# Attention and two feed-forward nets on one core: the head's chunks, weight fetches and one weight's last two steps rearranged

## The chip, the core and the metric

One core of a Trainium2 chip runs one program. Its engines are TensorE (PE; its weight loads PEld), VectorE (DVE), ScalarE (ACT), GpSimd (POOL) and SyncE (SP), which issues nearly all of the transfers. The metric is the device time of one execution in microseconds (us); lower is better.

## The reference

```python
qn = q / (np.linalg.norm(q, axis=1, keepdims=True) + 1e-06)   # q, k, v: 1 x 6016 x 256
kn = k / (np.linalg.norm(k, axis=1, keepdims=True) + 1e-06)
s = kn.transpose(0, 2, 1) @ qn / tau                          # 256 x 256
a = softmax(s, -1)
x = v @ a                                                     # 6016 x 256
h = x @ w_in                                                  # 256 -> 2048
g = where(h >= 1, h, where(h <= -1, 0, (h + 1) ** 2 / 4))
x = g @ w_out                                                 # 2048 -> 256
xn = x / sqrt(mean(x * x, -1) + 1e-06) * rms_g
out = (silu(xn @ w_gate) * (xn @ w_val)) @ w_out2             # 256 -> 1536 -> 256
```

The weights are float64 in memory; q, k and v are float32.

## The kernel before

**The head** reads q and k once. The 6016 tokens are 47 rows of 128, read in chunks (`QK_CHUNKS`, L24), each by one transfer of q and one of k (`load_chunk`, L364). For each row PE makes two fp32 products of 256 columns (`scores`, L353; halves b = 0 and 1 of the 256 x 256 score matrix); the trace has two records for each. In the same time the sums of squares of q and k are made: ACT squares a chunk (step `q5` of the table `HEAD`; `head_step`, L378), DVE adds the squares into the four rows of `acc` (`+5`, L400); at the end two folds, `<2` and `<1` (L405), leave one row, and four small products with a column of ones (`norm_ps`, L444) sum it over the partitions.

The head also turns the first three pieces of `w_in` (`wide`, 512 KB each; `fetch` after the chunks named by `FETCH_AT`) from float64 to a float32 pair, high and low part. A piece takes seven steps, written in `HEAD` as digit and letter: `c` clamp (DVE, L245), `h` shift (ACT, L252), `s` sign (DVE, L262), `r` rescale (ACT, L269), `j` join (DVE, L282), `u` high part (ACT, L321), `l` low part (DVE, L177). `2j 2u 2l` are the last three of the third piece. `HEAD` is the order of DVE and ACT in the head, `SCORES` that of PE, and each engine works its list strictly in order.

**Behind the head** a list scheduler at the end of the function orders everything, by costs and due times of its own: first the chain of the softmax (`softmax`, L570). ACT takes the square root of the norms (`norms_q`, L586), DVE the reciprocal and a diagonal matrix `rq` (L594), PE multiplies it out (`rq_ps`, L599), then come scaling, exponential, transposes and the product of the attention matrix with `w_in` (`product_w1`, L785), so that `v` goes straight into `x @ w_in` (`block_A`, L819; matmuls L830). The piece `s_ps` of the scores is copied by ACT (`s_sb`, L602) just ahead of `norms_q`. The scheduler starts with one clock for each engine (L1376), its assumption of when the engine is free of the head.

**The first net** (`block_A`, `squared`, `block_B`) follows at once, while the rest of the weights is still being turned: `soon`, the three pieces whose transfers go first after the head, and `wide_...`. In `squared` ACT and DVE make `g` from `h`, ACT the high part `gh`, DVE the low part `gl`; `block_B` multiplies both with `wo`, a piece of `w_out` with its own high and low part (`to_rows`, L718), in three matmuls: `gh` with the high part, `gh` with the low part, `gl` with the high part. A low part (`low`, L532; recorded as L177, `sub_hi`) can also be given to POOL, where the scheduler expects it to end earlier there than on DVE and the due time is below `SWAP_UNTIL`. From then on the same pattern goes through six pairs of token tiles and both nets.

Of the kernel before, what the change touches and what calls it, by code (L numbers as in the profile page):

```python
# [8 lines left out]
F32 = mybir.dt.float32  # L9
# [7 lines left out]
P = 128  # L17
TOK = 512
# [2 lines left out]
QK_BUFS = 8  # L21
SQ_BUFS = 3

QK_CHUNKS = (2, 2, 4, 4, 4, 4, 4, 4, 4, 4, 4, 3, 2, 2)  # L24
OWN = 2
ROWS = 4

WARM = 4
FILL = 12.0
NORM_AFTER = (11, 1)  # L30
SCORES = (
    (0, 0), (0, 1), (1, 0), (1, 1), (2, 0), (2, 1), (3, 0), (3, 1), (4, 0), (4, 1), (5, 0), (5, 1),
    (6, 0), (6, 1), (7, 0), (7, 1), (8, 0), (9, 0), (8, 1), (10, 0), (11, 0), (9, 1), (12, 0),
    (13, 0), (10, 1), (11, 1),
)
HEAD = (
    "q0 q1 q2 +2 q3 +3 0h 0c q4 0s 0r +4 1h 0j q5 1c 1s 0u +5 q6 1r 0l 2h +6 q7 1j 2c 1u +7 q8 1l +8 "
    "q9 2s +9 2r t q10 2j T 2u +10 q11 2l +11 q12 +12 q13 +13 <2 <1"
).split()

EARLY = 3
FETCH_AT = (3, 4, 6)

ORDER = ((1, 0), (1, 1), (2, 0), (1, 2), (2, 1), (1, 3), (2, 2), (1, 4), (2, 3), (1, 5), (2, 4), (2, 5))
PAIR = (1.5, 16.5)
# [46 lines left out]
def tile_channel_attention_two_ffn(  # L92
# [128 lines left out]
    def load_v(t):  # L221
        v_in[t] = op_slot(5 + t, [P, NC, TOK], F32, f"vin{t}")
        n0, n = tiles[t]
        nc.sync.dma_start(
            out=by_token(v_in[t]), in_=v[0, n0:n0 + n, :].rearrange("(m p) c -> p m c", p=P))
# [191 lines left out]
    with in_order(ENG.PE, ENG.DVE, ENG.Activation, ENG.SP):  # L417
        keep_warm(WARM)
        for ci in range(NQ):
            old = ci - QK_BUFS  # L420
            if 0 <= old and ci < NQ - OWN:
                for todo, upto, do in (
                    (steps, f"q{old}", head_step), (products, (old, 1), lambda w: scores(*w)),
                ):
                    while upto in todo:
                        do(todo.pop(0))
            load_chunk(ci)
            if ci == 0:
                nc.scalar.activation(out=seen, in_=ones[:, :1], func=AF.Sqrt)
            if ci == NQ // 2:  # L430
                nc.sync.dma_start(out=tau_sb, in_=tau.broadcast_to([P, 1]))
            if ci in FETCH_AT:
                fetch()
        load_v(0)
        load_v(1)
        while steps:
            head_step(steps.pop(0))
        sums = acc[:, :, 0]
        while products:
            scores(*products[0])  # L440
            if products.pop(0) == NORM_AFTER:
                for a in range(2):
                    for b in range(NC):
                        nc.tensor.matmul(  # L444
                            norm_ps[a][:, 2 * b:2 * b + 2], sums[:, a, b * P:(b + 1) * P],
                            ones[:, :2], start=True, stop=True,
                        )
    sent = {}
    for i, src in zip((2, 3, 4), SOON):
        x = op_slot(i, [P, NC, TOK], F32, f"soon{i}")  # L450
        sent[id(src)] = i, x

# [90 lines left out]
    def given(cls, name, slot, t, when=0.0):  # L543
        b = Buf(cls, name, slot=slot)
        b.t, b.when = t, when
        held.append(b)
        return b
# [92 lines left out]
        return ([rq_ps, rq_ps], mx_b[1:] * NC, s_b[0]), ([rq_ps, mx_b[1]], (), None)  # L640

    w1_part = Buf(None, "w1")

    vt_buf = {(t, c): Buf(None, f"vt{t}_{c}") for t in range(2) for c in range(NC)}
    for b, x in zip(vt_buf.values(), (s_all[1][1], s_all[0][0], warm, s_all[1][0])):
# [34 lines left out]
    def narrow(key, src, at, step, into=None):  # L680
        x = Buf("op", f"wide_{key}", [P, NC, TOK])
        low, high = (x, 0), (x, 1)
        if id(src) in sent:
            i, t = sent[id(src)]
            x = given("op", x.name, i, t, -10.0)
            low, high = (x, 0), (x, 1)
            op("SP", (0.5, 1.5), lambda: dma_wide(x.t, src), i - 100.0, writes=[low, high])
        else:
            op("SP", dma(512), lambda: dma_wide(x.t, src), at - LEAD["wide"], writes=[low, high], new=[x])
        small = pool(TOK * POOL_TS_NS / 1000)  # L690
        op("DVE", dve_fast(TOK), lambda: clamp(x.t), at, writes=[high],
           other=None if id(src) in sent else ("POOL", small, lambda: clamp(x.t, nc.gpsimd)))
        op("ACT", act(TOK), lambda: shift_act(x.t), at, writes=[low],
           other=("DVE", dve_fast(TOK), lambda: shift_dve(x.t)))
        op("DVE", dve(TOK), lambda: sign(x.t), at + step, [high], [low])
        op("ACT", act(TOK), lambda: rescale(x.t), at + step, [low], [high],
           other=("DVE", dve_fast(TOK), lambda: rescale_dve(x.t)))
        if into is None:
            op("DVE", dve(TOK), lambda: join(x.t), at + 2 * step, [high], [low])
        else:  # L700
            op("DVE", dve(TOK), lambda: join(
                x.t, into.t[:, :4, :].rearrange("p s c -> p (s c)")),
                at + 2 * step, [low, high], [(into, s) for s in range(4)], [into])
        return x
# [666 lines left out]
    for o in order:  # L1371
        o.new = [b for b in {id(b): b for b, _, _ in o.uses}.values() if b.cls and b.t is None]
        for b in o.new:
            if b not in queue[b.cls]:
                queue[b.cls].append(b)
    clock = {"PE": 1.2, "ACT": -2.6, "DVE": 0.0, "POOL": 0.0, "SP": -10.0}  # L1376
    dma_free = -4.9
    pending = {e: [] for e in clock}
    for o in order:
# [177 lines left out]
```

## Time and profile before

| | |
|---|---|
| median of three runs | 1098.97 us (1098.47 to 1099.27) |
| profiled execution, its own time | 1098.53 us |
| its span | 1096.7 us |
| DVE busy | 840.8 us, 77% |
| ACT busy | 799.8 us, 73% |
| POOL busy | 107.5 us, 10% |
| DMA over the span | 204.36 MB, 186 GB/s |

A row of the timeline has start, length (both us), engine, line, operation, what it writes and reads with shapes, and in brackets the idle time just before it and what ended that. Matmuls overlap, so the distance of two starts tells their pace, not their length. The page counts PE as busy nearly throughout; what matters is when it waits and in which order the other engines reach what it waits for.

### The profile page before, as it was taken

The page shows a single profiled execution, that of the slowest core. Times are in us where ns is not written, and L with a number is a line of the kernel's source. Part 1 is how long each engine was busy: PE and PEld are TensorE (multiplying, and loading weights), DVE is VectorE, ACT ScalarE, POOL GpSimd, SP SyncE. Part 2 cuts the span into 40 slices and gives each one's busy share as a digit, 9 for nine tenths or more (in the row PEclk, how much of TensorE's full clock was granted, in tenths as well). Part 3 has the DMA queues.
Part 4 walks back from the last instruction along what each step waited for, and adds up shares of the span by engine and source line. Part 5 has one row for each costly group of instructions (what it writes and reads, how often), then busy time and mean ns, then how long its engine had stood idle before and what let it go on. Part 6 is the DMA issues. An engine that isn't in the chain of part 4 may idle for free.

```text
span 1096.7 us, 14304 instructions
## 1 busy us (share of the span) xinstructions
PE 1090.2 (99%) x5038; PEld 923.2 (84%) x5038; DVE 840.8 (77%) x1342; ACT 799.8 (73%) x1454; POOL 107.5 (10%) x116
## 2 busy tenths in 40 slices
PE   9999999999999999999999999999999999999998
PEld 7888888888888888888888888998888888998887
DVE  5999999969999568867667967667967666866454
ACT  7799998877679776667877657887556877565553
POOL 0022213304222002000000200000100000200000
PEclk9999999999999999999999999999999999999999
DMA  9993576845688744446554445765455534455531
GB/s 360 368 304 124 184 256 232 226 155 198 218 302 240 197 158 133 163 170 194 149 152 163 150 169 132 231 174 170 143 172 129 196 135 167 159 179 161 187 115 39
DMA packets 130519, 204.36 MB, mean 186 GB/s; under 512 B 87184, under 2 KB 89232, under 8 KB 130448
## 3 DMA queue, kind: packets, MB, share of 16 engines
q1 hardware_dynamic: 129760, 202.80, 57.6%
q8 instruction: 40, 0.66, 0.2%
q10 hardware_dynamic: 688, 0.66, 0.2%
q14 instruction: 31, 0.25, 0.1%
HBM read 171.57 MB, written 31.85 MB: 185 GB/s over the span
## 4 chain that ended last, share of the span: by engine, by line
PE 97%; DMA 2%; DVE 1%; SPq 0%; issue 0%; DVEq 0%
PE y L868 23%; PE o L1091 14%; PE gx L989 9%; PE vx L989 9%; PE h L830 8%; PE hx L989 8%; PE gy L989 4%; PE vy L989 4%; PE hy L989 4%; PE o L1099 3%; PE s_ps L356 2%; PE vz L989 2%; PE gz L989 2%; PE hz L989 2%; DMA qk<-in_k_dram 2%; PE w_ps L798 1%
## 5 line engine op out<-in xcount | busy, mean ns | idle before, releaser
L868 PE MATMUL y<-gh,wo 128*128 128x512 f32 (+1 forms) x768 | 233.5, 385 | 0.0
L868 PEld LDWEIGHTS y<-gh,wo 128*128 128x128 f32 x768 | 144.2, 188 | 27.1
L177 DVE TENSOR_TENSOR gl<-g,gh 128x512 fp32r<-128x512 f32 (+1 forms) x190 | 128.0, 679 | 28.3 <-ACT gh L529 28.2
L868 PE MATMUL y<-gl,wo 128*128 128x512 f32 (+1 forms) x384 | 148.0, 385 | 0.0
L1091 PE MATMUL o<-uh,wd 128*128 128x512 f32 (+1 forms) x480 | 145.6, 385 | 0.0
L847 ACT ACTIVATE g<-g 128x512 f32<-128x512 f32 (+1 forms) x192 | 117.8, 620 | 1.6
L529 ACT ACTIVATE gh<-g 128x512 fp32r<-128x512 f32 (+1 forms) x192 | 116.9, 618 | 0.1
L1091 PEld LDWEIGHTS o<-uh,wd 128*128 128x128 f32 x480 | 90.1, 188 | 16.7
L1091 PE MATMUL o<-ul,wd 128*128 128x512 f32 (+1 forms) x240 | 92.2, 384 | 0.0
L868 PEld LDWEIGHTS y<-gl,wo 128*128 128x128 f32 x384 | 72.1, 188 | 13.8 <-DVE gl L177 0.4
L915 POOL TENSOR_SCALAR m<-sb 128x16 f32<-128x16 f32 (+1 forms) x12 | 5.1, 422 | 587.3 <-DVE sb L913 587.1
L989 PE MATMUL vx<-xb,vw 128*128 128x512 f32 (+1 forms) x216 | 60.2, 387 | 0.1
L989 PE MATMUL gx<-xb,gw 128*128 128x512 f32 (+1 forms) x216 | 60.1, 386 | 0.0
L989 PE MATMUL vx<-xt,vw 128*128 128x512 f32 (+1 forms) x216 | 59.9, 386 | 0.0
L989 PE MATMUL gx<-xt,gw 128*128 128x512 f32 (+1 forms) x216 | 59.9, 385 | 0.0
L989 PE MATMUL vy<-xt,vw 128*128 128x512 f32 (+1 forms) x216 | 59.9, 385 | 0.0
L989 PE MATMUL gy<-xt,gw 128*128 128x512 f32 (+1 forms) x216 | 59.8, 385 | 0.0
L1002 DVE TENSOR_TENSOR hc<-hy,hc 128x512 f32<-128x512 f32 (+1 forms) x32 | 21.5, 673 | 45.6 <-PE hy L989 45.6
L989 PE MATMUL hx<-vt,hw 128*128 128x512 f32 (+1 forms) x192 | 52.8, 383 | 0.0
L989 PE MATMUL hy<-vt,hw 128*128 128x512 f32 (+1 forms) x192 | 52.8, 383 | 0.0
L177 DVE TENSOR_TENSOR ul<-s,uh 128x512 fp32r<-128x512 f32 (+1 forms) x70 | 47.8, 684 | 6.4 <-ACT uh L529 6.2
L989 PE MATMUL hx<-vb,hw 128*128 128x512 f32 (+1 forms) x192 | 52.5, 383 | 0.0
(235 smaller groups left out, 2476.2 us busy)
## 6 DMA issues: line engine op xcount, KB each, us to landing
gw<-kept_g SPq DMA_DIRECT2D x36, 896.0 KB, 4.5
vw<-kept_v SPq DMA_DIRECT2D x36, 896.0 KB, 4.7
hw<-kept_h SPq DMA_DIRECT2D x32, 896.0 KB, 4.7
wo<-kept_wo SPq DMA_DIRECT2D x40, 512.0 KB, 4.1
wd<-kept_wd SPq DMA_DIRECT2D x36, 512.0 KB, 3.5
qk<-in_q_dram SPq DMA_DIRECT2D x9, 512.0 KB, 9.0
qk<-in_k_dram SPq DMA_DIRECT2D x9, 512.0 KB, 9.0
vin<-in_v_dram SPq DMA_DIRECT2D x32, 128.0 KB, 5.6
```

Source lines behind the costliest of these rows:

```text
L177: return eng.tensor_tensor(out=dst_lo, in0=src, in1=hi.bitcast(F32), op=ALU.subtract)
L356: nc.tensor.matmul(s_ps[b], x[:, 1, j, b * P:(b + 1) * P], x[:, 0, j, :], start=(ci == 0 and j == 0), stop=(ci == NQ - 1 and j == nj - 1),)
L529: op("ACT", act(n), lambda: nc.scalar.activation(out=hi(), in_=src(), func=AF.Copy), at, reads, writes, new, urgent, ("DVE", dve_fast(n), ...
L798: nc.tensor.matmul(got[b].t[:, :n], x[:, c * P:(c + 1) * P], w[:, c, cols], start=(j == 0), stop=(j == len(terms) - 1),)
L830: nc.tensor.matmul(ps.t[:, :n], w[:, c, f * P:(f + 1) * P], x[:, c, :n], start=(i == 0), stop=(i == len(terms) - 1),)
L847: op("ACT", act(n), lambda: nc.scalar.activation(out=r.t[:, :n], in_=r.t[:, :n], func=AF.Square), at, [], [r], urgent=rush)
L868: nc.tensor.matmul(y.t[c][:, :n], w.t[:, f % 2, h, cs], x[:, :n], start=(nth == 1 and i == 0), stop=(nth == NF1 and i == 2),)
L915: nxt("POOL", pool(0.3), lambda: nc.gpsimd.tensor_scalar(out=m.t[:, :nb], in0=s1.t[:, :n].rearrange("p (b j) -> p b j", j=32)[:, :, 0], sc ...
L989: nc.tensor.matmul(ps.t[:, :n], w.t[:, h, a, :], b.t[:, e, :n], start=(start and i == 0), stop=(i == 2), skip_group_check=True,)
L1002: op("DVE", dve(n), lambda: nc.vector.tensor_tensor(out=d.t[:, :n], in0=b.t[:, :n], in1=d.t[:, :n], op=ALU.add), at, [b], [d], urgent=20)
L1091: nc.tensor.matmul(o.t[c][:, :n], w.t[:, f % 2, h, cs], x[:, :n], start=(nth == 1 and i == 0), stop=(nth == NF2 and i == 2),)
L1099: nc.tensor.matmul(o.t[c][:, m * C:(m + 1) * C], x[:, (2 * c + m) * P:(2 * c + m + 1) * P], w.t[:, f % 2, h, :], start=(nth == 1 and i == ...
```

## The change

Four things, all of them numbers in tables or a moved call:

1. The first eight rows come as four chunks of two instead of 2, 2, 4. All later chunks shift by one index, which is most of the difference in `HEAD` and `SCORES`.
2. The three weight pieces are fetched after 16, 24 and 28 rows instead of 8, 12 and 20.
3. The third piece's `2j 2u` go to the end of `HEAD`, behind the folds, and its `2l` goes to the list scheduler, due at 5.0.
4. The first of the three `soon` pieces is sent between the two loads of `v`; the third gets a slot of its own (7). The scheduler's clock for DVE starts at 0.65 instead of 0.

```diff
-QK_CHUNKS = (2, 2, 4, 4, 4, 4, 4, 4, 4, 4, 4, 3, 2, 2)
+QK_CHUNKS = (2, 2, 2, 2, 4, 4, 4, 4, 4, 4, 4, 4, 3, 2, 2)
-    "q9 2s +9 2r t q10 2j T 2u +10 q11 2l +11 q12 +12 q13 +13 <2 <1"
+    "1u 2r q10 1l +10 q11 +11 t q12 +12 q13 +13 q14 T +14 <2 <1 2j 2u"
-FETCH_AT = (3, 4, 6)
+FETCH_AT = (5, 7, 8)
         load_v(0)
+        sent = {id(SOON[0]): (2, op_slot(2, [P, NC, TOK], F32, "soon2"))}
+        dma_wide(sent[id(SOON[0])][1], SOON[0])
         load_v(1)
-    sent = {}
-    for i, src in zip((2, 3, 4), SOON):
+    for i, src in zip((3, 7), SOON[1:]):
     w1_part = Buf(None, "w1")
+    last_wide = given("op", "last_wide", 4, fetched[-1][2], 0.0)
+    op("DVE", dve(TOK), lambda: early_step(EARLY - 1, "l"), 5.0, [last_wide],
+       [(w1_part, (2 * fetched[-1][0] + i, fetched[-1][1])) for i in range(2)])
-            x = given("op", x.name, i, t, -10.0)
+            x = given("op", x.name, i, t, -10.0 if i > 2 else -3.0)
-    clock = {"PE": 1.2, "ACT": -2.6, "DVE": 0.0, "POOL": 0.0, "SP": -10.0}
+    clock = {"PE": 1.2, "ACT": -2.6, "DVE": 0.65, "POOL": 0.0, "SP": -10.0}
```

How the instructions stand, at the three places that the prediction speaks of.

ACT at the end of the head, up to the square root of the norms, before (`wide1_0` is the third piece; L321 is its `2u`):

```order
22 L412 ACTIVATE spread_85<-ones_81,tau_sb_84 128x128
23 L321 ACTIVATE w1h_78<-wide1_0_143 128x512
24 L392 ACTIVATE sq11_257<-qk11_193 128x768 x2
25 L392 ACTIVATE sq12_262<-qk12_196 128x512 x2
26 L392 ACTIVATE sq13_266<-qk13_199 128x512 x2
27 L252 ACTIVATE soon2_342<-soon2_342 128x512
28 L602 ACTIVATE s_sb0_416<-s_ps0_0_107 128x256
29 L586 ACTIVATE norms_q_361<-norm0_ps_111 128x2
```

and now:

```order
25 L392 ACTIVATE sq14_271<-qk14_206 128x512 x2
26 L412 ACTIVATE spread_85<-ones_81,tau_sb_84 128x128
27 L321 ACTIVATE w1h_78<-wide1_0_156 128x512
28 L252 ACTIVATE soon2_211<-soon2_211 128x512
29 L252 ACTIVATE soon3_350<-soon3_350 128x512
30 L603 ACTIVATE s_sb0_423<-s_ps0_0_107 128x256
31 L587 ACTIVATE norms_q_368<-norm0_ps_111 128x2
```

Between the last square and `norms_q` there stood one shift and the copy; now `spread`, `2u`, two shifts and the copy stand there.

DVE at the same place, now (before, the folds were followed at once by the clamps of `soon`; L282 is `2j`):

```order
22 L400 TENSOR_TENSOR acc_106<-acc_106,sq10_253 128x2048
23 L400 TENSOR_TENSOR acc_106<-acc_106,sq11_258 128x2048
24 L410 RECIPROCAL tau_sb_84<-tau_sb_84 128x1
25 L400 TENSOR_TENSOR acc_106<-acc_106,sq12_263 128x2x768
26 L400 TENSOR_TENSOR acc_106<-acc_106,sq13_267 128x2x512
27 L400 TENSOR_TENSOR acc_106<-acc_106,sq14_271 128x2x512
28 L405 TENSOR_TENSOR acc_106<-acc_106 128x2x512
29 L405 TENSOR_TENSOR acc_106<-acc_106 128x2x256
30 L282 SCALAR_TENSOR_TENSOR wide1_0_156<-wide1_0_156 128x512
```

The adds follow one another without a step of a weight between them, and `2j` stands right behind the second fold.

The first `wo`: POOL's first subtractions (L177) behind its clamps, before:

```order
12 L177 TENSOR_TENSOR gl_2_655<-g_2_597,gh_2_641 128x512
13 L177 TENSOR_TENSOR wo_698<-soon_344,wo_698 128x2x256
14 L177 TENSOR_TENSOR gl_1_735<-g_1_664,gh_1_713 128x512
```

and now:

```order
12 L177 TENSOR_TENSOR wo_622<-soon_211,wo_622 128x2x256
13 L177 TENSOR_TENSOR gl_2_657<-g_2_597,gh_2_641 128x512
14 L177 TENSOR_TENSOR gl_1_735<-g_1_667,gh_1_716 128x512
```

The low part of the first `wo` (`wo0`, made from `soon2`) was DVE's (its row 71 before) and is now POOL's first subtraction. DVE's list up to the first `gl`, now:

```order
66 L854 SCALAR_TENSOR_TENSOR g0_2_597<-h0_2_572,g0_2_597 128x512
67 L262 SCALAR_TENSOR_TENSOR wide_wo2_425<-wide_wo2_425 128x512
68 L282 SCALAR_TENSOR_TENSOR soon3_350<-soon3_350 128x512
69 L262 SCALAR_TENSOR_TENSOR wide_wi20_427<-wide_wi20_427 128x512
70 L854 SCALAR_TENSOR_TENSOR g1_0_619<-h1_0_599,g1_0_619 128x512
71 L245 TENSOR_SCALAR wide_wo3_444<-wide_wo3_444 128x512
72 L177 TENSOR_TENSOR gl0_0_652<-g0_0_566,gh0_0_634 128x512
```

Before, `gl0_0` was row 72 as well, but with two clamps among the rows from 57 on, where there is now one. On ACT the high part of `wo0` stood behind the rescale of `soon3` and both steps of `g1_0`; now one of these, the square of `g1_0`, comes after it.

## Rows read from the trace of the kernel before

**Rows 1.** Page, part 1: busy time of each engine, share of the span, instructions.
```profile
PE 1090.2 (99%) x5038; PEld 923.2 (84%) x5038; DVE 840.8 (77%) x1342; ACT 799.8 (73%) x1454; POOL 107.5 (10%) x116
```

**Rows 2.** Waits of PE, whole span: total us, times, longest.
```profile
PE s_ps L356 <- DMA qk<-in_k_dram: 1.1, 2, 0.9
PE s_ps L344 <- DVE half L197: 1.0, 1, 1.0
```

**Rows 3.** Timeline of PE, head.
```profile
4.61 3.77 PE L356 MATMUL s_ps<-qk 128*128 128x256 f32 x16
9.31 10.60 PE L356 MATMUL s_ps<-qk 128*128 128x256 f32 x48 [0.94 <-DMA qk<-in_k_dram]
20.06 25.27 PE L356 MATMUL s_ps<-qk 128*128 128x256 f32 x116 [0.15 <-DMA qk<-in_k_dram]
45.28 1.02 PE L444 MATMUL norm_ps<-ones,acc 128*128 128x2 f32 x8
...
47.15 0.67 PE L599 MATMUL rq_ps<-rq,spread 128*128 128x256 f32 x2
```

**Rows 4.** Timeline of ACT: squares of k, rows 16 to 19 and 32 to 35.
```profile
19.95 1.06 ACT L392 ACTIVATE sq<-qk 128x1024 f32<-128x1024 f32 x1 [0.16 <-DMA qk<-in_k_dram]
...
31.55 1.06 ACT L392 ACTIVATE sq<-qk 128x1024 f32<-128x1024 f32 x1 [0.16 <-DMA qk<-in_k_dram]
```

**Rows 5.** Timeline of DVE, head.
```profile
20.00 0.43 DVE L245 TENSOR_SCALAR wide<-wide 128x512 f32<-128x512 f32 x1
20.54 0.70 DVE L262 SCALAR_TENSOR_TENSOR wide<-wide 128x512 uint32<-128x512 uint32 x1
...
35.93 2.28 DVE L400 TENSOR_TENSOR acc<-acc,sq 128x2048 f32<-128x2048 f32 x1
38.13 0.68 DVE L177 TENSOR_TENSOR w1l<-wide,w1h 128x512 fp32r<-128x512 f32 x1
38.73 4.41 DVE L400 TENSOR_TENSOR acc<-acc,sq 128x1536 f32<-128x1536 f32 x3
43.18 1.95 DVE L405 TENSOR_TENSOR acc<-acc 128x1024 f32<-128x1024 f32 x2
45.05 0.76 DVE L245 TENSOR_SCALAR soon<-soon 128x512 f32<-128x512 f32 x2
```

**Rows 6.** Timeline of ACT, end of the head.
```profile
43.42 0.70 ACT L252 ACTIVATE soon<-soon 128x512 uint32<-128x512 uint32 x1 [3.13 <-DMA soon<-in_moe_w_out_dram]
44.01 0.37 ACT L602 ACTIVATE s_sb<-s_ps 128x256 f32<-128x256 f32 x1
45.89 0.17 ACT L586 ACTIVATE norms_q<-norm_ps 128x2 f32<-128x2 f32 x1 [1.52 <-PE norm_ps L444]
```

**Rows 7.** Timeline of POOL, first net.
```profile
63.31 4.50 POOL L177 TENSOR_TENSOR gl<-g,gh 128x512 fp32r<-128x512 f32 x1 [12.54 <-ACT gh L529]
67.99 1.36 POOL L177 TENSOR_TENSOR wo<-soon,wo 128x512 fp32r<-128x512 f32 x1 [0.18 <-ACT wo L529]
...
92.40 2.59 POOL L752 TENSOR_TENSOR fg<-fg 128x128 f32<-128x128 f32 x1 [21.50 <-DVE fg L282]
```

**Rows 8.** Timeline of DVE, first net.
```profile
63.22 1.29 DVE L177 TENSOR_TENSOR gl<-g,gh 128x512 fp32r<-128x512 f32 x2
...
65.96 0.69 DVE L282 SCALAR_TENSOR_TENSOR soon<-soon 128x512 uint32<-128x512 uint32 x1
66.56 1.28 DVE L849 SCALAR_TENSOR_TENSOR g<-h,g 128x512 f32<-128x512 f32 x2
...
68.72 0.93 DVE L245 TENSOR_SCALAR wide_wi<-wide_wi 128x512 f32<-128x512 f32 x1
...
94.59 0.68 DVE L849 SCALAR_TENSOR_TENSOR g<-h,g 128x512 f32<-128x512 f32 x1
```

**Rows 9.** Timeline of ACT and of PE, the first `wo` and the first use of it.
```profile
60.98 0.68 ACT L529 ACTIVATE wo<-soon 128x512 fp32r<-128x512 f32 x1
...
63.31 0.62 PE L868 MATMUL y<-gh,wo 128*128 128x512 f32 x2
63.96 0.50 PE L868 MATMUL y<-gl,wo 128*128 128x512 f32 x1
```

More of the change, by code (lines that the diff above doesn't have):

```diff
@@ L29 @@
 FILL = 12.0
-NORM_AFTER = (11, 1)
+NORM_AFTER = (12, 1)
 SCORES = (
     (0, 0), (0, 1), (1, 0), (1, 1), (2, 0), (2, 1), (3, 0), (3, 1), (4, 0), (4, 1), (5, 0), (5, 1),
-    (6, 0), (6, 1), (7, 0), (7, 1), (8, 0), (9, 0), (8, 1), (10, 0), (11, 0), (9, 1), (12, 0),
-    (13, 0), (10, 1), (11, 1),
[2 rows of a table added]
 )
 HEAD = (
-    "q0 q1 q2 +2 q3 +3 0h 0c q4 0s 0r +4 1h 0j q5 1c 1s 0u +5 q6 1r 0l 2h +6 q7 1j 2c 1u +7 q8 1l +8 "
-    "q9 2s +9 2r t q10 2j T 2u +10 q11 2l +11 q12 +12 q13 +13 <2 <1"
+    "q0 q1 q2 +2 q3 +3 q4 +4 q5 +5 0h 0c 0s q6 0r +6 q7 0j 0u +7 1h 1c 0l 1s q8 +8 1r 2h 1j 2c 2s q9 +9 "
+    "1u 2r q10 1l +10 q11 +11 t q12 +12 q13 +13 q14 T +14 <2 <1 2j 2u"
 ).split()
 EARLY = 3
-FETCH_AT = (3, 4, 6)
+FETCH_AT = (5, 7, 8)
 ORDER = ((1, 0), (1, 1), (2, 0), (1, 2), (2, 1), (1, 3), (2, 2), (1, 4), (2, 3), (1, 5), (2, 4), (2, 5))
@@ L684, in narrow @@
             i, t = sent[id(src)]
-            x = given("op", x.name, i, t, -10.0)
+            x = given("op", x.name, i, t, -10.0 if i > 2 else -3.0)
             low, high = (x, 0), (x, 1)
-            op("SP", (0.5, 1.5), lambda: dma_wide(x.t, src), i - 100.0, writes=[low, high])
+            if i > 2:
+                op("SP", (0.5, 1.5), lambda: dma_wide(x.t, src), i - 100.0, writes=[low, high])
         else:
```

2 rows, old and new, of the table SCORES are left out of this document.

## The prediction

> **What bounds the kernel.** I began with the page's busy times: PE counts as busy for 1090.2 of 1096.7 us [rows 1]. A busy share can hide waiting, so the next view is PE's waits over the whole span: only the head has any, 1.1 us for k and 1.0 us before the first matmul [rows 2]. Behind the head PE runs without a gap worth naming, so a change here can give at most what PE loses in the head, and it can cost whatever new wait it makes. Third come the timelines of the four engines from the first chunk to the first net's first use of `wo`, where all the moved instructions stand.
>
> The sum is made against the profiled execution, 1098.53 us; its span is 1096.7. The median of the three runs is 0.44 us above it, and I add that at the end. A difference under 0.2% (2.2 us) is what a measurement of this kernel can't tell from none.
>
> **Term 1, PE in the head: 0.6 us earlier.** Ahead of the norm product PE has 16 + 48 + 116 = 180 records. The last 116 take 25.27 us, 0.218 each [rows 3], so 180 need 39.2 us; from 4.61 they would end at 43.8, yet the norm product starts at 45.28. Lost are 0.94 and 0.15 us for k, 0.28 in the first two chunks (16 records in 3.77 us against 3.49), and small change. With two-row chunks the first half of rows 4 to 7 has landed before PE wants it: the whole of them is there at 9.3 [rows 3], and PE reaches the second half only at about 10.1. The 0.94 goes. It is late again further on. Nine transfers of 512 KB lie between the landing of k for rows 16 to 19 and for rows 32 to 35, at 19.95 and 31.55 [rows 4], 1.29 us each. Rows 32 to 35 still have all three weights ahead of them, so their k still lands at 31.55; PE, unhindered, is there after 120 records, at 4.61 + 0.28 + 0.1 + 26.15 = 31.1, and waits 0.5. The last 60 records then end at 31.65 + 13.07 = 44.7, 0.6 before 45.28.
>
> **Term 2, DVE's folds: 0.7 us earlier, at 44.4.** Rows 16 to 19 have one weight less ahead of them: k lands at 19.95 - 1.29 = 18.7, its square takes 1.06 [rows 4], and the add starts at 19.8. From there DVE's list has no wait for data. Four adds followed by another kind of step take 2.20 each (35.93 to 38.13), 8.8; six joins, signs and low parts 0.60 each (38.13 to 38.73), 3.6; two clamps 0.54 each (20.00 to 20.54), 1.1; the three short adds 4.45 (38.73 to 43.18); the folds 1.95 [rows 5]. Two whole adds now stand before another add, which reads their result: 2.20 is the lower price, and the short ones lose 0.1 at each such step, so I take 2.36, together 4.7. The sum is 24.6, so the folds end at 44.4 instead of 45.13. `2j` and `2l`, 1.2 us, have left this list; an idle stretch before the add of rows 8 to 11 and the dearer adds take half of that back.
>
> **Term 3, ACT's list: 1.2 us later.** This turns the gain round. `2j` starts 0.08 before the folds end, as the clamp did before [rows 5], lasts 0.69 and ends at 45.0. `2u` waits for it, and behind `2u` on ACT stand two shifts of `soon`, the copy of the scores and only then `norms_q`, for which PE has been ready since about 45.3. A shift started 0.59 before the copy behind it [rows 6]; three such steps after 45.04 put the copy at 46.8 and `norms_q` at 47.1 (the copy, 0.37 long, lets the next one start 0.3 later). Before, ACT waited 1.52 us for PE and ran `norms_q` at 45.89 [rows 6]. From `norms_q` to `rq_ps` (47.15 [rows 3]) and on, each step waits for the one before it, so 1.2 us goes through to the first matmul of the net. The clock for DVE in the scheduler was raised for `2j`, ACT's was not for `2u`. The second shift's data is not what is late: the first `soon` landed at 43.4 [rows 6], and the second now lands one transfer later, 44.7, against 46.2 when ACT gets to it. `spread`, moved behind the last square, ends before `2j` does and costs nothing. The second load of v is put off by one transfer, to about 43.4, and its transposes come behind the norm product: nothing.
>
> **Term 4, the first `wo`: 0.75 us later.** All times here are on the clock of before; both sides have moved by term 3. ACT made the high part of `wo0` at 60.98 [rows 9]; now one step fewer stands ahead of it, so 60.45 to 61.13, and POOL gets its low part at 61.3 (0.18 after ACT, as at 67.99 [rows 7]). PE wants it at 63.54, one matmul after 63.31 [rows 9]. Is 2.2 us enough for POOL? The same subtraction took 1.36 us at 67.99 and 4.50 at 63.31 [rows 7]. At 63.31 DVE was running subtractions and joins with both inputs in SBUF, until 66.65; then it took a `g` step with one input from PSUM at 66.56, and POOL was done at 67.81, 1.16 after that join's end. At 92.40 a small one of 128 columns took 2.59 and ended at 94.99, just after DVE went over to a `g` step at 94.59 [rows 7, 8]. So POOL stands still while DVE goes from one such step to the next. In the new order DVE's first `gl` comes at 63.46 by the counts (one clamp less, one longer step more than before, where it was 63.22 [rows 8]); counted back by 0.60 and a clamp, `g1_0` runs at 62.5 and ahead of it a sign, a join and a sign, the last of them until 62.6. POOL, ready at 61.3, gets through at 62.6 and ends at 62.6 + 1.16 = 63.8. DVE's clamp behind `g1_0` then waits for POOL, as the clamp at 68.72 did, which ended 0.30 after POOL [rows 8]; the first `gl` starts at 64.0, ends at 64.65, and the third matmul comes at 64.7 instead of 63.96 [rows 9]. That is 0.75. The ends of this cost: 0.24 if POOL doesn't touch DVE; 4.7 if it misses `g1_0` and waits for the next `g` step, four subtractions or joins on, near 67.
>
> The 4.50 can also be read as a price of POOL's first subtraction, whichever engine is beside it. The Trainium skill, "SBUF — State Buffer", section "Who interferes with whom", says that DVE and GpSimd share a pair of SBUF ports, and that a DVE instruction with two SBUF inputs shuts out a GpSimd instruction that reads SBUF until it is done. By that rule the sum has 0.75 here; without it, and with a dear first use, 2.3. The row at 92.40, no first use and yet 2.59, agrees with the rule.
>
> **The sum.** Term 3 already holds terms 1 and 2; with term 4 it is 1.2 + 0.75 = 1.95 us: 1098.53 + 1.95 = 1100.5 for a profiled execution, with the 0.44 to the median **1100.9**, 0.18% slower. With the folds between 43.9 and 44.9 and term 4 between 0.24 and 1.5 the case runs from 1099.9 to 1102.1.
>
> **The rivals.**
> - *ACT is not late.* If DVE ends its folds by 42.4, `2u` and the shifts are over when PE's norm product is, and term 1 counts: -0.6, with term 4 +0.15. For it: DVE has 1.2 us less to do. Against it: DVE would have to start the add of rows 16 to 19 two us before its data is there. 1098.4 to 1099.2, not slower; chance 0.13. Even with no wait at all PE could gain only 1.5, so faster by over 0.2% is hardly to be had.
> - *POOL's first subtraction is dear in itself.* 61.3 + 4.5 = 65.8 against 63.54, so 2.3 in place of 0.75: 1102.5. It decides if POOL's first L177 lasts over 4 us with a `g` step of DVE inside. Chance 0.12.
> - *POOL is shut out past `g1_0`.* It would need DVE to be 0.5 us ahead of my count, so that `g1_0` is over when POOL asks. Then 1.2 + 4.7: 1104.9. Chance 0.08.
> - *The chunks don't do what they say.* If 256 KB transfers run slower than 512 KB ones, all landings move back: 0.3 to 0.5 on terms 1 and 2, within the forecast's range.
>
> **How the numbers follow.** The forecast has 0.62, the three rivals 0.33; 0.05 is left for stalls further on. DVE and ACT have no slack up to 100 us and a third subtraction (`gl1_3`) goes to POOL, but PE's delay gives them two us more. The bound of 2.2 us, 1101.2, cuts the forecast's own range: a third of it lies above. Slower by over 0.2%: 0.62/3 + 0.12 + 0.08 + 0.02 = 0.42. Faster: 0.03. Within 0.2%: 0.55. The range 1098.9 to 1103.0 takes in the forecast, most of the first rival and the second, and leaves out the third.
>
> **What would show it.** In the profile of the changed kernel: the gap of 0.94 at 9.3 gone and one of about 0.5 on PE near 31.1; the folds' end near 44.4; on ACT `2u`, two shifts and the copy without a gap, then `norms_q` near 47.1, with PE idle for nearly 2 us between `norm_ps` and `rq_ps`; POOL's first L177 lasting about 2.5 us and ending as DVE's `g1_0` does; PE's first `gl` matmul about a second stall. The forecast is wrong if `norms_q` waits for PE, as before, or if POOL's step ends before PE asks for it.

## The result, and the profile after

The changed kernel takes 1105.14 us (median of six runs, 1102.30 to 1106.34), the kernel before beside it 1098.89 (1098.39 to 1099.27): a ratio of 1.0056 with a 95% interval of 1.0043 to 1.0069, 0.56% slower. The forecast was 0.18% slower, with a range up to 1103.0. The direction was right; more than two thirds of the loss were not in the forecast. Five of the six runs have a mean granted clock of TensorE of 0.997 or 0.998 and take 1105.14 to 1106.34; the sixth, at 1.000, took 1102.30.

The profiled execution of the changed kernel took 1105.14 us, its span 1103.4, that is 6.7 more than before. First PE's waits over the whole span, which before were two, both in the head [rows 2]:

```profile
PE rq_ps L600 <- DVE norms_k L582: 1.6, 1, 1.6
PE y L873 <- DVE gl L177: 1.5, 1, 1.5
PE s_ps L356 <- DMA qk<-in_k_dram: 1.1, 1, 1.1
PE s_ps L344 <- DVE half L197: 1.0, 1, 1.0
PE y L873 <- POOL wo L177: 0.2, 1, 0.2
```

Two waits are new, 1.6 us before `rq_ps` and 1.5 before the first `gl` matmul, and together with the 0.2 they come to 3.3 us. That is half of 6.7. The timeline of PE shows the other half, beside [rows 3]:

```profile
7.38 37.83 PE L356 MATMUL s_ps<-qk 128*128 128x256 f32 x172 [1.06 <-DMA qk<-in_k_dram]
45.04 0.95 PE L446 MATMUL norm_ps<-ones,acc 128*128 128x2 f32 x8
...
48.57 1.19 PE L600 MATMUL rq_ps<-rq,spread 128*128 128x256 f32 x2 [1.61 <-DVE norms_k L582]
49.55 1.91 PE L356 MATMUL s_ps<-qk 128*128 128x256 f32 x4
...
56.67 0.40 PE L835 MATMUL h<-vh,w1h 128*128 128x512 f32 x1
...
66.32 0.39 PE L873 MATMUL y<-gh,wo 128*128 128x512 f32 x1
66.89 0.50 PE L873 MATMUL y<-gh,wo 128*128 128x512 f32 x1 [0.19 <-POOL wo L177]
68.86 0.69 PE L873 MATMUL y<-gl,wo 128*128 128x512 f32 x1 [1.47 <-DVE gl L177]
```

`rq_ps` itself takes 1.19 us instead of 0.67 [rows 3], and four records of the scores behind it 1.91, where before they took 1.03. PE works at half pace there. The windows of the changed kernel say so (columns: stretch, its length, busy us and instructions of PE, PEld, DVE, ACT and POOL, granted TensorE clock, DMA share, GB/s):

```profile
45.00:47.00 2.00, 1.96 (x13) 1.48 (x12) 0.59 (x2) 1.71 (x4) 0.00 (x0) 1.00 1.05 400
47.00:49.00 2.00, 0.43 (x1) 0.46 (x2) 1.40 (x6) 1.94 (x6) 0.85 (x2) 0.88 1.04 380
49.00:51.00 2.00, 2.00 (x6) 1.55 (x6) 1.00 (x5) 0.48 (x2) 1.17 (x2) 0.50 1.06 382
51.00:53.00 2.00, 2.00 (x15) 1.80 (x14) 1.09 (x5) 0.90 (x5) 0.00 (x0) 0.76 1.10 347
53.00:65.00 12.00, 12.00 (x70) 10.40 (x69) 11.43 (x24) 11.33 (x24) 0.65 (x1) 1.00 1.05 266
65.00:70.00 5.00, 3.35 (x12) 2.22 (x11) 5.00 (x8) 5.00 (x11) 3.26 (x2) 0.90 1.23 204
70.00:80.00 10.00, 10.00 (x40) 8.09 (x40) 10.00 (x18) 7.74 (x15) 2.15 (x1) 0.88 0.81 264
```

Read PE's busy time together with the granted clock: PE is busy for 0.43 of 2 us from 47 to 49, and from 49 to 51 the granted clock is 0.50, the lower of its two levels, 1.2 GHz. It happens again: PE is busy for 3.35 of 5 us from 65 to 70, and the clock of the next ten is 0.88. In the kernel before it was 1.00 in all of these stretches; two of them, before:

```profile
49.00:51.00 2.00, 2.00 (x21) 2.00 (x19) 1.76 (x7) 1.36 (x6) 1.11 (x2) 1.00 1.05 377
70.00:80.00 10.00, 10.00 (x46) 8.29 (x45) 10.00 (x17) 10.00 (x20) 0.91 (x1) 1.00 1.01 348
```

So the loss has four parts, two waits and two stretches at a lower clock. Set against the times of before, the first `h` matmul comes 3.08 us later (56.67 against 53.59), the first `gl` matmul 4.90 later (68.86 against 63.96 [rows 9]), the end 6.7 later.

Behind the first wait stands ACT's list, as forecast (beside [rows 6]):

```profile
45.29 0.68 ACT L321 ACTIVATE w1h<-wide 128x512 fp32r<-128x512 f32 x1 [5.20 <-DVE wide L282]
45.87 1.21 ACT L252 ACTIVATE soon<-soon 128x512 uint32<-128x512 uint32 x2
46.98 0.36 ACT L603 ACTIVATE s_sb<-s_ps 128x256 f32<-128x256 f32 x1
47.25 0.15 ACT L587 ACTIVATE norms_q<-norm_ps 128x2 f32<-128x2 f32 x1
```

Behind the second stand POOL and DVE (beside [rows 7, 8]):

```profile
64.36 2.49 POOL L177 TENSOR_TENSOR wo<-soon,wo 128x512 fp32r<-128x512 f32 x1 [13.58 <-DMA wide_wo<-in_moe_w_out_dram]
66.81 1.45 POOL L177 TENSOR_TENSOR gl<-g,gh 128x512 fp32r<-128x512 f32 x1
```

```profile
65.59 0.68 DVE L854 SCALAR_TENSOR_TENSOR g<-h,g 128x512 f32<-128x512 f32 x1
66.19 0.94 DVE L245 TENSOR_SCALAR wide_wo<-wide_wo 128x512 f32<-128x512 f32 x1
67.05 2.36 DVE L177 TENSOR_TENSOR gl<-g,gh 128x512 fp32r<-128x512 f32 x2
```

POOL's low part of `wo0` ends at 66.85. Its next subtraction, the low part of `gl0_2`, is in the queue and starts at 66.81. DVE's first two `gl` take 2.36 us instead of 1.29 [rows 8]. The first of them, for which PE waits, takes 1.76 of that (67.05 to 68.81) and ends 0.55 after POOL's subtraction (68.26); the second takes 0.68. It looks as if POOL, which DVE had held up, now holds up DVE; a run further down tests this.

### The profile page after: what moved, and what is told of

Its sections match the earlier page's. It is cut to its first block, busy times and chain, and to the rows that moved or that the text cites. A ratio compares the mean times of both kernels' runs of the same rounds, so it can differ in the third digit from the quotient of the medians.

```text
span 1103.4 us, 14310 instructions
## 1 busy us (share of the span) xinstructions
PE 1093.4 (99%) x5038; PEld 925.4 (84%) x5038; DVE 841.9 (76%) x1342; ACT 802.4 (73%) x1456; POOL 103.3 (9%) x117
## 4 chain that ended last, share of the span: by engine, by line
PE 93%; DMA 3%; DVE 2%; ACT 1%; issue 0%; SPq 0%; DVEq 0%; ACTq 0%
PE y L873 23%; PE o L1096 14%; PE gx L994 9%; PE vx L994 9%; PE hx L994 8%; PE h L835 7%; PE gy L994 4%; PE vy L994 4%; PE hy L994 4%; PE o L1104 3%; PE vz L994 2%; PE gz L994 2%; DMA qk<-in_q_dram 2%; PE hz L994 2%; DMA qk<-in_k_dram 1%; PE w_ps L803 1%
## 5 line engine op out<-in xcount | busy, mean ns | idle before, releaser
L177 DVE TENSOR_TENSOR gl<-g,gh 128x512 fp32r<-128x512 f32 (+1 forms) x189 | 130.1, 693 | 27.4 <-ACT gh L530 27.2
L177 DVE TENSOR_TENSOR ul<-s,uh 128x512 fp32r<-128x512 f32 (+1 forms) x70 | 47.9, 684 | 6.4 <-ACT uh L530 6.2
```

The costliest lines, as they stand in the source:

```text
L177: return eng.tensor_tensor(out=dst_lo, in0=src, in1=hi.bitcast(F32), op=ALU.subtract)
```

## The experiments

Theory A: PE's two waits cost their length, and each can put PE's clock on its lower level, which costs as much again; the first comes from `2u` standing ahead of `norms_q` on ACT, the second from POOL. The rivals: the waits alone are the loss, and the chain hides the clock; or the loss lies in the chunks and transfers. The results of added matmuls on ones and of the added subtraction are used by nobody. Each group of four ran beside its own runs of the kernel before.

**PE kept busy in the first wait.** (The edits of the experiments are shown shortened.)

```diff
+            keep_warm(3)
             nc.tensor.matmul(rq_ps.t[:, :C], spread, rq.t[:, :C], start=True, stop=True)
```

> The changed kernel with three matmuls on data that is long there (ones by ones, into a PSUM bank that is overwritten later) put on PE just ahead of rq_ps, where PE stood idle for 1.61 us in the changed kernel; nothing else differs. Theory A (the granted clock is the missing cost: PE's 1.6 us of idleness at 47 to 48.6 us is followed by 3 to 4 us at the 1.2 GHz level, and that costs 1.7 us beside the wait itself): granted clock 1.00 from 47 to 53 us, rq_ps still at about 48.6 but 0.67 us long instead of 1.19, first h matmul at about 55.0 instead of 56.67, median 1103.4 against the 1105.1 of the changed kernel. Theory B (the chain through DVE and ACT after norms_q sets the pace anyway, the clock costs nothing): first h matmul still at 56.4 to 56.7, median 1105. Theory C (the lower clock comes from the few columns of the norm product, not from the wait): clock still falls, median 1105.

Measured: 1102.60 us (before: 1098.70), ratio 1.0031 (1.0019 to 1.0042). Windows of this run, then its PE:

```profile
47.00:49.00 2.00, 1.63 (x8) 1.16 (x7) 1.39 (x6) 1.95 (x6) 0.82 (x2) 1.00 1.04 374
49.00:51.00 2.00, 2.00 (x16) 1.82 (x15) 1.53 (x8) 0.60 (x2) 1.26 (x2) 1.00 1.05 384
...
65.00:70.00 5.00, 3.35 (x14) 2.49 (x14) 5.00 (x8) 4.44 (x10) 1.63 (x2) 1.00 1.06 226
70.00:80.00 10.00, 10.00 (x46) 8.15 (x45) 10.00 (x18) 9.78 (x19) 2.18 (x1) 1.00 0.81 280
```

```profile
46.78 1.46 PE L344 MATMUL s_ps<-ones 128*128 128x256 f32 x6
48.60 0.67 PE L602 MATMUL rq_ps<-rq,spread 128*128 128x256 f32 x2 [0.37 <-DVE norms_k L582]
...
55.04 0.40 PE L837 MATMUL h<-vh,w1h 128*128 128x512 f32 x1
```

`rq_ps` starts as late as before (48.60 against 48.57), but with the clock at 1.00 the first `h` comes 1.63 us earlier. That is the price of the first clock drop, with the wait itself left in place; theories B and C fall. The median fell by more, 2.5, since the second drop is mostly gone too: the wait at the first `gl` is there unchanged (PE busy 3.35 of 5 us), with a clock of 1.00 behind it. So that wait does not always bring the drop. Nor does a drop need it: of the 23 runs of the kernel before beside this group two had a mean clock of 0.998 and 0.997 and took 1101.19 and 1101.04, the others at most 1099.45. The profile of that kernel has a clock of 1.00, so where it fell in those two isn't known.

**ACT's `2u` put behind the copy of the scores.**

```diff
-"... +14 <2 <1 2j 2u"
+"... +14 <2 <1 2j"
+    op("ACT", act(TOK), lambda: early_step(EARLY - 1, "u"), 4.0, [last_wide], last_part)
```

> The changed kernel with one ACT instruction moved: the third weight's high part (2u) stands behind the copy of the scores instead of ahead of the two soon shifts; every other engine's order is the same. Theory A (ACT's late 2u causes PE's first wait, and the wait causes the clock drop): the two shifts and the copy run before 2j is done, norms_q at about 46.1 instead of 47.25, PE waits under 0.5 us before rq_ps, granted clock 1.00 from 45 to 53, first h matmul at about 53.6 (as in the kernel before) instead of 56.67; the second wait, at the first wo, stays, since DVE, POOL and PE move together: median about 1102.0. Theory B (only the wait, not the clock): first h at 55.5, median 1104. Theory C (DVE's list is what is late, and 2u merely waits with it): norms_q hardly earlier, median 1105.

Measured: 1102.51 us, ratio 1.0030 (1.0020 to 1.0039). PE's wait before `rq_ps` is 0.5 and the clock 1.00 from 45 to 53, as theory A has it. The loads of q and k landed late in the profiled execution (norm product at 46.78); from there to the first `h` it took 8.88 us, against 11.63 in the changed kernel and 8.31 before. The wait at the first `gl` is still 1.5. The median, 3.81 us above the kernel before, is hardly below that of the run with the wait filled (3.90), though in the profiles the way from the norm product to the first `h` is 1.1 us shorter (8.88 against 10.02): with landings that move, and four of the nine runs at a mean clock of 0.998, these two medians don't show the length of the wait. The run with ACT's clock set right and the one with both waits filled, below, show it together.

**The low part of `wo0` on DVE.**

```diff
+        if (kind, j) == ("wo", 0):
+            ops[-1].other = None
```

> The changed kernel with the low part of wo0 kept on DVE (its alternative on POOL taken away; the list schedule behind it then also moves some steps of later blocks). The head is untouched: norms_q at 47.25, PE's wait of 1.6 us, the lower clock and first h at 56.67 stay. Theory A (POOL's subtraction of wo0, with POOL's next one shutting DVE out, is the cause of PE's 1.5 us wait, and that wait of the second clock drop): no wait at the first y, first gl matmul 0.65 us after the first y matmul as in the kernel before (now 2.5), granted clock 1.00 from 65 to 80, median about 1101.5 (1.9 for the wait and 1.8 for the clock). Theory B (the wait goes, the clock drop there has another cause or costs nothing): median about 1103.2. Theory C (DVE has no room for it, PE waits for DVE's gl all the same): median 1104.5 to 1105.5.

Measured: 1101.96 us, ratio 1.0027 (1.0017 to 1.0037). PE no longer waits for `gl`, and the clock from 65 to 80 is 1.00. The head's wait of 1.6 stays. The eight runs show the clock's price once more: five with a mean granted clock of 1.000 have spans of 1099.3 to 1100.4, three with 0.998 have 1101.2 to 1102.3, 2.0 us more on average, with the same instructions. The order that makes the head's wait is the same in all eight, so that wait too does not seem to bring the drop every time.

**The scheduler told when ACT is free.** One number takes both causes away, since the schedule then gives `wo0`'s low part back to DVE by itself.

```diff
-    clock = {"PE": 1.2, "ACT": -2.6, "DVE": 0.65, ...
+    clock = {"PE": 1.2, "ACT": 0.85, "DVE": 0.65, ...
```

> The changed kernel with one number changed: the list scheduler is told that ACT is busy until 0.85 us (when 2u ends) instead of -2.6. It then puts norms_q straight behind 2u, the soon shifts far later, and by itself gives wo0's low part back to DVE. Theory A (both waits of PE and both clock drops come from the scheduler's not knowing of 2u): norms_q at about 46.0, first h at about 53.5, no wait at the first y unless the shifts of soon are now too late for wo0, clock 1.00 everywhere, median 1098.3 to 1099 (no slower than the kernel before). Theory B (waits only): 1101.8. Theory C (the soon shifts put off delay wo0's join and PE waits at the first y): first y matmul waits 1 to 2 us, median 1100 to 1102.

Measured: 1099.36 us, ratio to the kernel before 1.0005 (0.9996 to 1.0014): of the 6.25 us above the kernel before 0.7 are left (1099.36 against 1098.70). PE's only waits are in the head, 0.2 before `rq_ps`; the clock is 1.00 from 43 to 1000 us. It is as fast as the kernel before, not faster.

```profile
47.67 0.67 PE L600 MATMUL rq_ps<-rq,spread 128*128 128x256 f32 x2 [0.17 <-DVE norms_k L582]
...
54.12 0.40 PE L835 MATMUL h<-vh,w1h 128*128 128x512 f32 x1
```

**One part of the change at a time.** First the chunks and fetches with the third weight's steps back among the adds, then the steps behind the folds with the chunks and fetches of before. Of each edit the line of `HEAD` is shown; the place of the third piece's low part and the scheduler's clock for DVE go with it, in the second the slot 7 too.

```diff
-... 1l +10 q11 +11 t q12 +12 q13 +13 q14 T +14 <2 <1 2j 2u
+... 1l +10 t q11 2j T 2u +11 q12 2l +12 q13 +13 q14 +14 <2 <1
```

> The two-row chunks and the later fetches alone: the changed kernel with the third weight's join, high and low part back among the adds of the head, as in the kernel before (join and high part ahead of the add of chunk 11, low part ahead of that of chunk 12). DVE then has its 1.2 us back ahead of the folds, so these end at 45.9 where the loads land as in the profile of the changed kernel, and the norm product follows; ACT has nothing late. Theory A (neither part is bad by itself, the loss comes from 2j and 2u behind the folds together with POOL's subtraction): no wait over 0.5 us before rq_ps, no wait at the first y, clock 1.00, first h at about 54.3, median 1099.0 to 1099.8. Theory B (the chunks and fetches themselves cost, by late data or transfers): median above 1101.

```diff
-    "q9 2s +9 2r t q10 2j T 2u +10 q11 2l +11 q12 +12 q13 +13 <2 <1"
+    "q9 2s +9 2r t q10 T +10 q11 +11 q12 +12 q13 +13 <2 <1 2j 2u"
```

> The join behind the folds alone: the kernel before with 2j and 2u moved behind the folds, 2l in the list schedule, DVE's clock of the scheduler at 0.65 and the third soon tile in slot 7; chunks and fetches as before, the three soon tiles loaded by the list schedule as before. Here only one soon shift stands between 2u and the copy of the scores, and the schedule leaves wo0's low part on DVE. DVE's folds end 1.2 us earlier, at 43.9, 2u at 45.2, shift and copy at 46.1, norms_q at 46.3 instead of 45.89. Theory A: 0.4 us, no clock drop, no wait at the first y: median 1099.0 to 1099.5. Theory B (moving 2u behind the folds is the fault whatever the chunks): norms_q at 47, PE waits 1.2 us or more and the clock falls: 1101.5 to 1102.5.

Measured: 1099.80 us, ratio 1.0010 (1.0001 to 1.0019), and 1099.93, ratio 1.0011 (1.0002 to 1.0019). Each part alone costs a tenth of a per cent; together they cost 0.56%. In the first, with `2j` and `2l` back on DVE ahead of the folds, these end at 46.48 and PE waits 0.5 us for them, and for nothing behind. In the second, with one shift between `2u` and the copy, PE's wait before `rq_ps` was 1.1 us, where 0.4 us was expected for the whole delay, and the clock stayed at 1.00:

```profile
48.71 0.67 PE L599 MATMUL rq_ps<-rq,spread 128*128 128x256 f32 x2 [1.09 <-DVE rq L594]
```

**Is it POOL's next subtraction that holds DVE up?** The kernel with PE busy in the first wait, and `gl0_2` kept on DVE.

```diff
+        if (t, f) == (0, 2):
+            ops[-1].other = None
```

> The kernel of e1_warm_head (the changed one with PE kept busy ahead of rq_ps), in which the low part of gl0_2 stays on DVE; wo0's low part stays on POOL, and the list schedule moves some steps of later blocks. In e1 POOL's gl0_2 started at 65.19, as soon as wo0's low part was done, and DVE's first two gl took 2.36 us (65.43 to 67.79) instead of 1.28. Theory A (POOL's next subtraction, already in its queue, gets the memory ahead of the waiting DVE: 1.07 us of PE's wait of 1.5): the two gl take about 1.3 us, PE's wait for gl is about 0.4, the first gl matmul comes 1.4 us after the first y matmul instead of 2.5, median about 1101.5 against 1102.6. Theory B (wo0's low part on POOL is all there is to it, gl0_2 stands beside it): two gl still 2.3, median 1102.6.

At the place in question theory A holds. DVE's three `gl` take 1.88 us, PE's wait falls from 1.5 to 0.39, and from the first `y` matmul to the first `gl` one there are 1.45 us instead of 2.5:

```profile
66.10 1.88 DVE L177 TENSOR_TENSOR gl<-g,gh 128x512 fp32r<-128x512 f32 x3
```

The time went the other way: 1103.84 us, where 1101.5 was expected. The schedule behind it has other steps on POOL (`wo1`'s low part too). DVE's steps beside them at 71.58, 73.01 and 83.04 take 1.50, 1.52 and 1.78 us, where steps of their kind take 0.68, 0.42 and 0.68 undisturbed, and PE waits again 20 us later. From the first `gl` matmul to the end this run takes 2.4 us longer than the one it is built on, and most of that lies here: PE's 23 records from 85.47 take 7.25 us, where the pace just before them, 0.227 each, would give 5.2. A further 0.67 of the difference between the two spans is a norm product that starts later (45.69 against 45.02).

```profile
87.02 0.50 PE L837 MATMUL h<-vh,w1h 128*128 128x512 f32 x1 [0.94 <-DVE g L856]
```

**PE kept busy in the second wait, then in both, and the changed kernel again.** The second wait is filled in `block_B`:

```diff
+                if (t, f, c, i) == (0, 0, 0, 2):
+                    for _ in range(3):
+                        nc.tensor.matmul(s_all[1][1]..., ones, wide_ones, start=True, stop=True)
```

> The changed kernel (head as it is, with its wait of 1.6 us and its low clock) with three matmuls on ones put on PE ahead of the first gl matmul, where it waits 1.5 us; every other order is the same. Theory A (the lower clock at 67 to 80 us comes from that wait): granted clock 1.00 from 65 to 80, first gl matmul still 2.5 us after the first y matmul, median 1105.1 - 1.8 = 1103.3. Theory B (the second drop comes from the head's, the wait at the first y has nothing to do with it; in e1_warm_head and e5_high_part_back the same wait of 1.5 us had a clock of 1.00 behind it): clock of 65 to 80 still below 1, median 1105.

> The changed kernel with three matmuls on ones at both places where PE stood idle, ahead of rq_ps and ahead of the first gl matmul: all waits of the other engines stay, PE only is not idle in them. Theory A (the loss is 1.36 us of norms_q, 1.9 us at the first y and some 3 us of lower clock behind both): first h at 55.0, first gl matmul 2.5 us after the first y matmul, clock 1.00 in every run, no run above 1103.2, median 1102.2 (1098.9 + 3.3). Theory B (something else further on is slower in the changed kernel too): median stays at 1103.5 to 1105.

> The changed kernel once more, without an edit, on the chip of e10_warm_both. It measures how much of its time hangs on the chip and on the lower clock. Theory A: runs whose mean granted clock is 1.000 take 1101.5 to 1102.5, runs with 0.998 or less 1103.3 to 1106.3, median 1104 to 1105.3, 1.5 to 3 us above e10_warm_both. Theory B (the clock's mean has nothing to do with the time): both kinds of runs have the same times, and the median is that of e10_warm_both.

Measured: second wait filled 1103.64 us (beside 1098.90); both filled 1102.84 (1102.48 to 1103.26, beside 1098.55); the changed kernel again, on the same chip as the latter, 1104.31 (1102.99 to 1105.93). With the second wait filled the clock from 65 to 80 is 1.00, and the head's drop is as it was. In the profiles of the last two, the stretch from 49 to 51 and that from 70 to 80 read, both filled first:

```profile
49.00:51.00 2.00, 1.68 (x9) 1.18 (x7) 1.61 (x7) 1.24 (x2) 1.16 (x2) 1.00 1.05 373
...
70.00:80.00 10.00, 10.00 (x45) 8.17 (x44) 10.00 (x18) 9.21 (x18) 2.18 (x1) 1.00 0.87 293
```

```profile
49.00:51.00 2.00, 1.64 (x4) 1.40 (x5) 1.19 (x6) 0.79 (x2) 0.82 (x2) 0.57 1.05 374
...
70.00:80.00 10.00, 10.00 (x39) 8.02 (x39) 10.00 (x19) 7.67 (x15) 2.16 (x1) 0.84 0.87 281
```

Filling the waits with useless work makes the kernel 1.5 us faster at the median, with five runs each whose ranges just overlap. The five runs of the changed kernel fall in order of their mean clock: 0.999 took 1102.99, 0.998 took 1104.23 and 1104.31, 0.997 took 1105.75 and 1105.93. So the clock costs 1.5 at the median and 3 where both drops fall. The rest is 4.3 us (1102.84 against 1098.55), where 3.3 was expected. The waits make 3.6 of it: from the norm product to the first `h` it takes 9.98 us here and 8.31 before, from the first `y` matmul to the first `gl` one 2.53 and 0.65. The other 0.7 is what the run with ACT's clock set right, which has neither wait, had lost too. Filling the second wait as well gave no more than filling the first alone (3.90 above the kernel before), which fits the clock of 1.00 behind the second wait in that run's profile.

**Is POOL's first subtraction dear in itself?** The kernel before with an added one at the very start.

```diff
+    first = const.tile([P, P], F32, name="first")
+    nc.gpsimd.tensor_tensor(out=first, in0=ones, in1=ident, op=ALU.subtract)
```

> The kernel before with one more subtraction on POOL (ones minus ident, 128x128, result unused) right behind the constants, when DVE has no step with two SBUF inputs; POOL's first L177 at 63.31, which took 4.50 us, then is no longer its first subtraction. Theory A (POOL is shut out by DVE's steps with both inputs in SBUF): the added one takes under 0.6 us, the subtraction at 63.3 still 4.4 to 4.5. Theory B (a first subtraction is dear in itself): the one at 63.3 takes 1.2 to 1.5. Time of the whole as before, 1098.4 to 1099.3.

```profile
1.37 0.46 POOL L458 TENSOR_TENSOR first<-ones,ident 128x128 f32<-128x128 f32 x1
...
63.81 4.50 POOL L177 TENSOR_TENSOR gl<-g,gh 128x512 fp32r<-128x512 f32 x1 [12.66 <-ACT gh L531]
```

The added one takes 0.46, the one at 63.81 still 4.50 [rows 7], and the whole 1098.92 (one run; before: 1098.55). It is not the first use. The changed kernel says the same: there POOL's first subtraction took 2.49.

**A try at a faster one, which failed.** The fetches one to two chunks later still, on top of the ACT clock; `HEAD` changes with them.

```diff
-FETCH_AT = (5, 7, 8)
+FETCH_AT = (6, 8, 10)
```

> The kernel of e2_act_clock with the three weights fetched one, one and two chunks later (behind rows 20, 28 and 36) and their steps in the lists of the head put off to match. If the head is bound by the landing of q and k that the weights are in front of, rows 16 to 19 and 32 to 35 land 1.3 us earlier each, PE's wait of 0.6 us at 32 us goes, DVE's folds end about 1 us earlier (44.2 where e2 had 45.2) and the first h comes at 53.3 to 53.6 against 54.12: median 1098.3 to 1098.8 against 1099.36, no slower than the kernel before. If DVE's list is the bound and its steps only change places: folds as before, median 1099.2 to 1099.5. If a weight now lands too late for its own steps in DVE's list: above 1100.

Measured: 1108.95 us, ratio 1.0091 (1.0077 to 1.0105). PE waits 6.5 us for the folds, and the granted clock is 0.50 from 51 to 53. I had written the high parts (`u`) on ACT ahead of the next squares; each waits for DVE's join, the squares behind it come late, and DVE's next add waits for those, 2.6 us at a time:

```profile
26.46 0.67 ACT L321 ACTIVATE wi<-wide 128x512 fp32r<-128x512 f32 x1 [2.11 <-DVE wide L282]
```

```profile
29.05 2.29 DVE L400 TENSOR_TENSOR acc<-acc,sq 128x2048 f32<-128x2048 f32 x1 [2.62 <-ACT sq L392]
```

This says nothing on whether later fetches could help; a list for them that keeps ACT's squares first was not tried.

## Why the prediction was wrong, step by step

- **Term 3 (ACT's list, 1.2 us): right.** `norms_q` at 47.25 where 47.1 was forecast, behind `2u`, two shifts and the copy without a gap, 1.36 us later than before. The run with `2u` moved and the one with ACT's clock corrected leave 0.5 and 0.2 us of PE's wait.
- **The sum (1.2 + 0.75): here it failed.** The prediction says that a change "can cost whatever new wait it makes", and expects PE to be idle for nearly 2 us, but it counts the wait as its length and nothing else. The granted clock after the wait was 0.50, and that cost another 1.63 us in the head, shown by the run that fills the wait with work; with the second drop it is 3 us where both fall, 1.5 at the median on the second chip. The kernel before had a clock of 1.00 behind the head and no wait of PE there, so a wait of nearly 2 us was outside what its trace showed. The Trainium skill, "TensorE: Matmul & The Clock Gate", section "HAM oscillation — how this bites in real kernels", says that a wait of PE between two groups of matmuls can let its clock fall back. The traces agree with that, by the 0.50 behind the wait and the 1.00 with the wait filled, but 1.61 us is shorter than the waits in that section's example, and the measurement decides.
- **Term 4 (the first `wo`, 0.75 us): mechanism right, too small.** POOL's subtraction took 2.49 us (2.5 forecast) and got through when DVE's `g1_0` ran, at 65.59. PE's first `gl` matmul came 1.82 us later than term 3 and the clock explain (4.90 - 3.08). The step that failed is "the first `gl` starts at 64.0, ends at 64.65". Put back by the 3.08 us of the first delay, it started at 63.97, as forecast, but lasted 1.76 us and ended at 65.73: the prediction let DVE go on as soon as POOL had finished one subtraction, but POOL's next was queued and went first. With that one on DVE, 1.45 us lay between the first `y` and the first `gl` matmul, where the prediction had 1.4 (64.7 - 63.31) and the changed kernel 2.54. The rule cited in the prediction (the Trainium skill, "SBUF — State Buffer", section "Who interferes with whom") also has it that whichever of the two issues first keeps the ports for a whole instruction; the `gl` that started 0.24 after POOL's subtraction and ended 0.55 after it agrees, and I had applied it in one direction only.
- **Term 1 (PE's scores, 0.6 us earlier): mis-sized.** The norm product started at 45.04, 0.24 earlier. The gap of 0.94 at 9.3 came back as one of 1.06 at 7.38, for the second chunk of k, but that is not what decided: in the run with the first wait filled PE had no gap so early, and the norm product started at 45.02. The step that failed is "their k still lands at 31.55". PE began with rows 32 to 35 at 32.02, in the nine profiles that have this head between 32.00 and 33.76, and the norm product started 13.0 us after that in each (the prediction's 13.07). So it started between 45.02 and 46.78, on average at 45.8; in the three with the chunks and fetches of before at 45.28, 45.70 and 45.78. The chunks alone made nothing faster (1099.80).
- **Term 2 (DVE's folds, 44.4): nearly.** They ended at 44.65, and `norms_q` started 2.6 us after that, where the prediction had 2.7. In the seven profiles with this order on ACT it is 2.57 to 2.61, so a late landing delays the folds and `norms_q` with them.
- **The rivals.** "ACT is not late" is refuted by the 47.25. "POOL's first subtraction is dear in itself" is refuted by the added one. "POOL is shut out past `g1_0`" did not happen, though its 1104.9 is close to what was measured. That its number is close is luck. A lower clock stood among none of them; without it (1102.84 with both waits filled) the time would have been inside the range, which ended at 1103.0.

Put together for the profile, whose end is 6.7 us later: term 3 gave 1.36, the way from there to the first `h` 1.72 (1.63 of it the clock, by the run that fills the wait), the first `wo` 1.82, and 1.8 came between the first `gl` matmul and the end. Of the last, 0.2 to 0.3 is there as well in the three profiles of filled waits, whose clock was 1.00 behind the first `gl`, so about 1.5 is the clock. For the median it is 6.25 us against 1.95 forecast: 0.7 that stays without either wait, 3.6 for the length of the two waits, and 2.0 for the clock, where the chip of the last group gave 1.5. The 0.7 is not clear of noise (ratio 0.9996 to 1.0014), and what it is made of stays open. Why the wait of 1.5 us at the first `gl` was followed by the lower clock in the two profiles of the changed kernel, and not in those with the first wait filled or shortened, stays open.

## What to carry to other kernels

Price a new wait of a busy PE twice: its length, and the half pace that can come behind it (here in most runs, not in all), read from the granted clock in the windows and not from the list of waits; and if the wait can't be removed, useless matmuls in it give part of the loss back. When a step moves to the end of an engine's list, the scheduler's clock of every engine that then waits for it should move too: here one number, ACT's, took the loss from 6.25 us to 0.7. And where POOL and DVE both work from SBUF, ask what POOL has queued behind the instruction that DVE waits for: here one more subtraction went ahead of DVE's step.

## What the hardware showed that I had not expected

- One wait of 1.61 us of PE, behind some small products, was followed by a stretch at 0.50 (1.2 GHz). A wait of 1.09 us at the same place was followed by 1.00.
- The same 1.5 us wait at the first `gl` was followed by a clock of 0.88 in one kernel and 1.00 in another. It is a matter of chance in part: of eight runs of the kernel with `wo0`'s low part on DVE, three had the lower mean clock and took 2.0 us longer.
- A DVE clamp of 0.42 us took 0.94 and one `gl` 1.76 instead of 0.68 beside a POOL subtraction each: the two engines hold each other up in both directions.
- The landing of q and k moves the end of the head by up to 1.8 us from one profiled execution to the next (45.02 to 46.78), as much as any of the terms argued over here; behind the k of rows 32 to 35 the rest of the head took 13.0 us every time.
